# A feed-forward block on one core: w1's first piece on ScalarE's queue, the rest of w1 on SyncE's behind the table load, the bias by software DMA

## The chip, the cores and the metric

The kernel runs on one core of a Trainium2 chip. The metric is the device time of a run in microseconds (us), median over runs.

## The reference

Activations of 2048 tokens by 448 features go through a two-layer feed-forward block with a tanh-approximated GELU between the layers, all in bf16:

```python
def reference(x, w1, b1, w2, b2):
    h = jnp.einsum("bsd,df->bsf", x, w1) + b1      # x: 1 x 2048 x 448, w1: 448 x 1792
    h = _gelu(h)
    return jnp.einsum("bsf,fd->bsd", h, w2) + b2   # w2: 1792 x 448
```

## The kernel before, in words

The 2048 tokens are worked through in four chunks of 512. For each chunk, layer 1 computes the hidden features transposed (features on partitions, tokens along the row), in 14 feature tiles of 128, two tiles to a pair, so seven pairs. ScalarE adds the bias and applies GELU while it moves each tile from PSUM to the SBUF buffer `g` (L267). Layer 2 then multiplies `g` with w2, token tile by token tile; VectorE adds b2 and SyncE stores the tile (L310, L273).

The contraction of layer 1 is 448 = 3 x 128 + 64. Every matmul works on 64 rows of the array, so two of them, one on the upper and one on the lower half, run at once. A pair's part "a" is 6 matmuls (three steps of 128 rows, one half for each of the two tiles), its part "b" 8: the other halves, and last the remainder step `k == KT` with the 64 rows that are left over. Those remainder rows of w1 lie in `w1r`, loaded into partitions 64 to 127 (`load_w1r`, L135 to L137); for the odd tile of each pair VectorE copies them to partitions 0 to 63 (L381, events "w1rU"), because there the other half of the array does the remainder step.

w1 arrives in pieces. `W1CUTS = (0, 4, 8, 14)` cuts its main 384 rows by feature tile: piece 0 holds tiles 0 to 3 (384 KB), piece 1 tiles 4 to 7 (384 KB), piece 2 tiles 8 to 13 (576 KB). `RCUTS = (0, 4, 14)` cuts the remainder rows: piece 0 holds tiles 0 to 3 (64 KB), piece 1 the rest (160 KB). In the first chunk the order of pairs is L0.a and L1.a (in two halves of 256 tokens), L0.b, L2.a, L1.b, L3.a, L2.b, L4.a, L3.b and so on. So TensorE needs first piece 0 of w1, at the end of L0.b piece 0 of the remainder rows, at L2.a piece 1 of w1, at the end of L2.b piece 1 of the remainder rows, at L4.a piece 2 of w1.

The first chunk of x comes as it is (`xn`, L153) and is turned by TensorE (L337, L358), with VectorE and ScalarE moving the results to `xT` (L344, L367). Until x is there, TensorE runs warm-up matmuls on constants (L190). The other three chunks come through transposing DMAs (L147).

The order of the work is written by hand. A small helper, `Program`, keeps one list of operations per engine: `op` appends a computation, `dma` a transfer, `barrier` a bare wait. Each operation has a list of events that it waits for and may carry an event that it fires when done; `emit` turns these into semaphores and writes the lists out, engine by engine, in their order. So on each queue everything stands behind what was appended before it, a wait included.

At the start the queues hold:

- SyncE: x; w1 piece 0; w1 piece 2; remainder rows 1; w2 in two halves; b2; twelve transposing loads of x.
- ScalarE: the bias b1 (L171, waiting for VectorE's memset of its buffer, L170); a dummy GELU (L173), in front of which the activation table is loaded; remainder rows 0; w1 piece 1; then its evacuations.
- GpSimd: the identity matrix for the turning (L165, L166) and a memset for layer 2's bias rows (L169).
- VectorE: the memset; the evacuations of x; `turn_b1`, four 32x32 transposes and a cast that bring b1 onto partitions (L179, L181); the two remainder copies (L381); then the additions of layer 2.

Of the kernel before, what the change touches and what calls it, by code (L numbers as in the profile page):

```python
# [5 lines left out]
ACT = mybir.ActivationFunctionType  # L6
# [67 lines left out]
def bass_standalone__dense_activation_gelu__prompt_kernel(  # L74
# [10 lines left out]
    P = 128  # L85
# [5 lines left out]
    NSC, NST, STC, NFT = S // SC, S // P, SC // P, F // P  # L91
# [6 lines left out]
    with ExitStack() as es:  # L98
# [8 lines left out]
        junk = sb("junk", [P, 1], BF16)  # L107
        b1n = sb("b1n", [32, P], BF16)
# [8 lines left out]
        pr = Program(nc, es)  # L117
        one = nc.const_aps.tensor(1.0, [P, 1], BF16)
# [9 lines left out]
        def load_w1(i, engine="sync"):  # L128
            c0, c1 = W1CUTS[i] * P, W1CUTS[i + 1] * P
            pr.dma(engine, lambda e: e.dma_start(  # L130
                w1_sb[:, :, c0:c1], w1[0:D3, c0:c1].rearrange("(k p) f -> p k f", p=P)), ("w1", i))
# [3 lines left out]
        def load_w1r(i, engine="sync"):  # L135
            cs = slice(RCUTS[i] * P, RCUTS[i + 1] * P)
            pr.dma(engine, lambda e: e.dma_start(w1r[H:P, cs], w1[D3:D, cs]), ("w1r", i))  # L137

        def load_w2(a, b):
            pr.dma("sync", lambda e: e.dma_start(  # L140
                w2_sb[:, a:b, :], w2[a * P:b * P, :].rearrange("(f p) d -> p f d", p=P)), ("w2", a))
# [9 lines left out]
        x0v = x2[0:SC, :].rearrange("(p t) d -> p t d", t=STC)  # L151
        o0v = out2[0:SC, :].rearrange("(p t) d -> p t d", t=STC)
        pr.dma("sync", lambda e: e.dma_start(xn[:, :, :], x0v), "x")  # L153
        load_w1(0)
        load_w1(2)
        load_w1r(1)
        load_w2(0, 7)
        load_w2(7, 14)
        pr.dma("sync", lambda e: e.dma_start(b2_bc[:, :], b2.partition_broadcast(P)), "b2")
        for c in range(1, NSC):  # L160
            for slot in range(KT + 1):
# [6 lines left out]
            base=0, pattern=[[-1, P]], channel_multiplier=1), after=["ident0"], event="ident")  # L168
        pr.op("gpsimd", lambda e: e.memset(b2_z[:, :], 0.0), event="b2z0")  # L169
        pr.op("vector", lambda e: e.memset(b1n[:, :], 0.0), event="b1z")  # L170
        pr.dma("scalar", lambda e: e.dma_start(b1n[0:NFT, :], b1.rearrange("(c p) -> c p", p=P)), "b1n",  # L171
               after=["b1z"])
        pr.op("scalar", lambda e: e.activation(junk[:, :], one, ACT.Gelu_apprx_tanh))  # L173
        load_w1r(0, "scalar")
        load_w1(1, "scalar")

        def turn_b1():
            for q in range(4):
# [216 lines left out]
        for c in range(NSC):  # L395
# [14 lines left out]
            p = Layer2(c, (0, 1))  # L410
# [46 lines left out]
```

## Time and profile before

| what | us |
|---|---|
| median of 3 runs | 99.45 |
| lowest, highest | 99.04, 99.66 |
| the profiled execution, its own time | 99.45 |
| its span, first to last instruction | 98.1 |
| TensorE matmul busy | 92.4 (94% of the span) |
| ScalarE busy | 38.6 (39%) |
| VectorE busy | 13.4 (14%) |
| GpSimd busy | 1.1 (1%) |

The profile is of one execution. "PE" is TensorE's matmul side and "PEld" its weight loads, "DVE" VectorE, "ACT" ScalarE, "POOL" GpSimd, "SP" SyncE; a "q" behind a name is the engine's sequencer, which issues the DMAs. An issue row's length is the time of the issuing alone; the time to landing is given apart. In the names, `w_sb` stands for `w1_sb` and `w2_sb`, `u` for the PSUM units, `b_bc` for the broadcast b2, `b_f` for the turned b1. The page's slices show TensorE's granted clock in tenths over 40 equal stretches; for this run it begins:

```profile
PEclk9999957999999999999999999999999999999999
```

The mean granted clock of the run is 0.982.

### The profile page before, as it was taken

What the parts mean: (1) busy time and instruction counts of PE and PEld (TensorE: products, weight loads), DVE (VectorE), ACT (ScalarE), POOL (GpSimd) and SP (SyncE); (2) the same over time, 40 slices, a digit from 0 to 9 for tenths busy, and PEclk for the clock granted to TensorE, in tenths of its full rate; (3) what the DMA queues carried; (4) which work ended last, traced back from release to release, by engine and by line L of the source; (5) the groups of instructions that cost most, each with busy time, mean ns of one, the idle gap of its engine ahead of it and who ended that gap; (6) DMA issues with size and microseconds to landing.
All of it is one profiled execution on the core that took longest, in us unless ns stands there. A gap on an engine that the chain in (4) does not pass through costs nothing.

```text
span 98.1 us, 2060 instructions
## 1 busy us (share of the span) xinstructions
PE 92.4 (94%) x932; PEld 47.2 (48%) x932; DVE 13.4 (14%) x33; ACT 38.6 (39%) x63; POOL 1.1 (1%) x7
## 2 busy tenths in 40 slices
PE   6995399999999999999999999999999999999990
PEld 2571133445555444445555444455554444466890
DVE  0271101100004500000033300000044000000421
ACT  3262253894000088990000389870000698930001
POOL 4000000000000000000000000000000000000000
PEclk9999957999999999999999999999999999999999
DMA  2989999655422210000002300000002200000022
GB/s 64 304 281 308 359 269 124 127 98 102 103 60 76 71 41 0 0 7 0 0 0 97 96 0 3 0 0 7 0 19 74 94 7 0 0 0 7 0 94 94
DMA packets 12340, 7.32 MB, mean 75 GB/s; under 512 B 6956, under 2 KB 12140, under 8 KB 12332
## 3 DMA queue, kind: packets, MB, share of 16 engines
q1 hardware_dynamic: 11824, 6.74, 28.4%
q10 hardware_dynamic: 508, 0.46, 1.6%
q8 instruction: 7, 0.11, 0.5%
q14 instruction: 1, 0.01, 0.0%
HBM read 3.79 MB, written 1.84 MB: 57 GB/s over the span
## 4 chain that ended last, share of the span: by engine, by line
PE 86%; DMA 9%; ACTq 1%; ACT 1%; DVE 1%; issue 0%
PE u L215 86%; DMA w_sb<-in_w_dram 9%; ACTq L171 1%; ACT L173 1%; DVE out_sb L324 0%; DVE b1n L170 0%
## 5 line engine op out<-in xcount | busy, mean ns | idle before, releaser
L267 ACT ACTIVATE g<-u,b_f 128x512 bf16<-128x512 f32 x56 | 35.0, 686 | 44.9 <-PE u L215 44.9
L215 PE MATMUL u<-xT,w_sb 64*128 64x512 bf16 (+1 forms) x348 | 42.3, 378 | 2.0 <-DMA w_sb<-in_w_dram 2.0
L215 PE MATMUL u<-w_sb,g 64*128 64x448 bf16 (+1 forms) x504 | 43.2, 328 | 0.0
L215 PEld LDWEIGHTS u<-w_sb,g 64*128 64x128 bf16 x504 | 24.5, 94 | 18.4
L215 PEld LDWEIGHTS u<-xT,w_sb 64*128 64x128 bf16 x348 | 17.2, 96 | 22.4 <-DMA w_sb<-in_w_dram 2.3
L310 DVE TENSOR_TENSOR out_sb<-u,b_bc 128x448 bf16<-128x448 f32 x14 | 8.1, 620 | 64.9 <-PE u L215 64.9
L215 PE MATMUL u<-xT,w1r 64*128 64x512 bf16 x56 | 11.3, 391 | 0.7 <-DMA w1r<-in_w_dram 0.7
L215 PEld LDWEIGHTS u<-xT,w1r 64*128 64x128 bf16 x56 | 2.9, 96 | 4.7 <-DMA w1r<-in_w_dram 1.2
L190 PE MATMUL u<-const-bfloat16-1.0 128*128 128x512 bf16 (+1 forms) x9 | 3.8, 579 | 0.8 <-PEq L442 0.8
L327 ACT CAST out_sb<-u 128x224 bf16<-128x224 f32 x1 | 0.3, 347 | 9.2 <-PE u L215 9.2
L190 PEld LDWEIGHTS u<-const-bfloat16-1.0 128*128 128x128 bf16 x9 | 1.2, 141 | 2.4 <-issue 2.4
L173 ACT ACT_TABLE_LOAD x1 | 1.3, 1283 | 1.6 <-DVE b1n L170 1.6
L344 ACT COPY xT<-u 128x384 bf16<-128x384 bf16 x2 | 1.0, 479 | 2.0 <-PE u L337 2.0
L337 PEld LDWEIGHTS u<-ident,xn 128*128 128x128 bf16 x12 | 1.2, 144 | 0.6 <-issue 0.6
L337 PE MATMUL u<-ident,xn 128*128 128x128 bf16 x12 | 1.4, 310 | 0.0
L185 DVE COPY xT<-xT 64x512 bf16<-64x512 bf16 x3 | 0.9, 290 | 3.5 <-DMA xT<-in_x_dram 3.4
L381 DVE COPY w1r<-w1r 64x256 bf16<-64x256 bf16 (+1 forms) x2 | 0.6, 288 | 3.1 <-DMA w1r<-in_w_dram 3.1
L318 DVE TENSOR_TENSOR out_sb<-u,b_bc 128x448 bf16<-128x448 f32 x1 | 0.6, 625 | 1.7 <-PE u L215 1.7
L179 DVE STREAM_TRANSPOSE b1t<-b1n 32x32 bf16<-32x32 bf16 x4 | 0.8, 202 | 0.1
L405 DVE COPY b_z<-b_bc 1x448 bf16<-1x448 bf16 x1 | 0.3, 267 | 4.0 <-DMA b_bc<-in_b_dram 4.0
L344 DVE COPY xT<-u 128x384 bf16<-128x384 bf16 x2 | 0.7, 358 | 0.7 <-PE u L337 0.7
L367 ACT COPY xT<-u 64x256 bf16<-64x256 bf16 x2 | 0.7, 368 | 0.1
(17 smaller groups left out, 4.1 us busy)
## 6 DMA issues: line engine op xcount, KB each, us to landing
out_dram<-out_sb SPq DMA_DIRECT2D x16, 112.0 KB, 1.7
w_sb<-in_w_dram SPq DMA_DIRECT2D x2, 784.0 KB, 10.9
w_sb<-in_w_dram SPq DMA_DIRECT2D x1, 576.0 KB, 8.4
xn<-in_x_dram SPq DMA_DIRECT2D x1, 448.0 KB, 3.2
w_sb<-in_w_dram SPq DMA_DIRECT2D x1, 384.0 KB, 4.3
w_sb<-in_w_dram ACTq DMA_DIRECT2D x1, 384.0 KB, 9.1
xT<-in_x_dram SPq DMA_TRANSPOSE x12, 3.6
w1r<-in_w_dram SPq DMA_DIRECT2D x1, 160.0 KB, 8.8
```

The costliest lines, as they stand in the source:

```text
L171: pr.dma("scalar", lambda e: e.dma_start(b1n[0:NFT, :], b1.rearrange("(c p) -> c p", p=P)), "b1n", after=["b1z"])
L173: pr.op("scalar", lambda e: e.activation(junk[:, :], one, ACT.Gelu_apprx_tanh))
L179: pr.op("vector", lambda e, q=q: e.transpose(b1t[32 * q:32 * q + 32, :], b1n[:, 32 * q:32 * q + 32]), after=["b1n"], event=("b1t", q))
L185: pr.op("vector", lambda e: e.tensor_copy(xT[0:H, KT, s0:s1], xT[H:P, KT, s0:s1]), after=after, event=event)
L190: pr.op("tensor", lambda e: e.matmul(unit[0][:, 0, 0:cols], lhsT=ones_w, rhs=ones_m[:, 0:cols], start=True, stop=True))
L215: o = pr.op("tensor", lambda e: e.matmul(unit[u][:, lo, cols], lhsT=lhsT, rhs=rhs, start=start, stop=stop, skip_group_check=skip), after=a ...
L267: pr.op("scalar", lambda e, lo=lo, ft=ft: e.activation(g[:, ft, c * SC:(c + 1) * SC], unit[u][:, lo, :], ACT.Gelu_apprx_tanh, bias=b1_f[:, ...
L310: pr.op("vector", lambda e, lo=lo, j=j: e.tensor_tensor(out=out_sb[:, j, :], in0=unit[u][:, lo, 0:D], in1=b2_bc[:, :], op=ALU.add), after= ...
L318: pr.op("vector", lambda e: e.tensor_tensor(out=out_sb[:, j, :].rearrange("p (two h) -> p two h", two=2), in0=unit[u][:, :, 0:DH], in1=b2_ ...
L337: pr.op("tensor", lambda e, k=k: e.transpose(stage(t)[:, k * P:(k + 1) * P], xn[:, t, k * P:(k + 1) * P], ident[:, :]), after=["ident", "x ...
L344: pr.op(engine, lambda e: e.copy(o, i) if engine == "scalar" else e.tensor_copy(o, i), after=[("xt", t)], event=("xT0", t))
L367: e.copy(o, i) if engine == "scalar" else e.tensor_copy(o, i),
```

## The change

x is still first on SyncE's queue. Behind it stands a wait for the event "table", which the dummy GELU on ScalarE now fires when it is done. Behind the wait come remainder rows 0, w1 piece 1, remainder rows 1, w1 piece 2, and then w2, b2 and the transposing loads as before. w1 piece 0 is issued from ScalarE's queue, behind the table load and the dummy GELU; the other two w1 transfers leave that queue. The bias is loaded by a DMA issued from GpSimd's queue, behind its three preparing operations, with the same wait for VectorE's memset. Nothing else is touched: the same bytes are loaded, and TensorE's order of work is the same.

```diff
         pr.dma("sync", lambda e: e.dma_start(xn[:, :, :], x0v), "x")
-        load_w1(0)
+        pr.barrier("sync", ["table"])
+        load_w1r(0)
+        load_w1(1)
+        load_w1r(1)
         load_w1(2)
-        load_w1r(1)
         load_w2(0, 7)
         load_w2(7, 14)
...
         pr.op("vector", lambda e: e.memset(b1n[:, :], 0.0), event="b1z")
-        pr.dma("scalar", lambda e: e.dma_start(b1n[0:NFT, :], b1.rearrange("(c p) -> c p", p=P)), "b1n",
+        pr.dma("gpsimd", lambda e: e.dma_start(b1n[0:NFT, :], b1.rearrange("(c p) -> c p", p=P)), "b1n",
                after=["b1z"])
-        pr.op("scalar", lambda e: e.activation(junk[:, :], one, ACT.Gelu_apprx_tanh))
-        load_w1r(0, "scalar")
-        load_w1(1, "scalar")
+        pr.op("scalar", lambda e: e.activation(junk[:, :], one, ACT.Gelu_apprx_tanh), event="table")
+        load_w1(0, "scalar")
```

## The prediction

> **What bounds the kernel now.** I read the chain of waits in order of time first. It names the one wait that sets the end:
>
> ```profile
> 2.23 9.07 DMA w_sb<-in_w_dram
> 11.30 0.05 issue
> 11.35 84.59 PE u L215 x877
> 95.94 0.38 DVE out_sb L324
> ```
>
> From 11.35 us on it is TensorE alone. What released it is the second piece of w1 (feature tiles 4 to 7), issued at 2.23 on ScalarE's queue, behind the bias and the first remainder rows, and landed 9.07 later at 11.30. Next, the timeline from 0 to 20 us (start, length, engine, line; not every row):
>
> ```profile
> 5.83 2.13 PE L215 MATMUL u<-xT,w_sb 64*128 64x256 bf16 x30
> ...
> 8.68 0.64 PE L215 MATMUL u<-xT,w1r 64*128 64x512 bf16 x2 [0.71 <-DMA w1r<-in_w_dram]
> ...
> 11.35 1.58 PE L215 MATMUL u<-xT,w_sb 64*128 64x512 bf16 x12 [2.03 <-DMA w_sb<-in_w_dram]
> ...
> 16.07 1.46 PE L215 MATMUL u<-xT,w_sb 64*128 64x512 bf16 x12
> ...
> 17.58 1.46 PE L215 MATMUL u<-xT,w_sb 64*128 64x512 bf16 x12
> ```
>
> Layer 1 starts at 5.83, runs out of operands at 7.96, gets the remainder rows at 8.68 and w1's second piece at 11.35. Then there is a second loss: 28 matmuls between 11.35 and 16.07 take 4.72, while the 14 from 16.07 take 1.51, so 28 should take 3.02. The table by windows says why (after the stretch and its length: busy time of PE, PEld, DVE, ACT, POOL; then granted clock, DMA share, GB/s):
>
> ```profile
> 12.50:13.00 0.50, 0.50 (x6) 0.19 (x4) 0.00 (x0) 0.00 (x0) 0.00 (x0) 0.58 1.08 377
> 15.50:16.00 0.50, 0.50 (x4) 0.15 (x2) 0.09 (x1) 0.00 (x0) 0.00 (x0) 0.51 1.40 275
> 16.00:16.50 0.50, 0.50 (x7) 0.20 (x4) 0.00 (x0) 0.23 (x1) 0.00 (x0) 1.00 4.32 56
> ```
>
> A mean of 0.58 in the first half microsecond means full speed for 0.08 of it (0.16 + 0.84 x 0.5 = 0.58): the clock halves at 12.58 and is back at 15.99, 3.41 later. In the 3.41 before 12.58 TensorE was busy only 0.15 + 1.23 = 1.38 (40%). So the wait for w1 costs its own idle time and 4.72 - 3.02 = 1.70 of half clock.
>
> The page's part on DMA issues gives the order of landing:
>
> ```profile
> w_sb<-in_w_dram SPq DMA_DIRECT2D x1, 576.0 KB, 8.4
> xn<-in_x_dram SPq DMA_DIRECT2D x1, 448.0 KB, 3.2
> w_sb<-in_w_dram SPq DMA_DIRECT2D x1, 384.0 KB, 4.3
> w_sb<-in_w_dram ACTq DMA_DIRECT2D x1, 384.0 KB, 9.1
> ...
> w1r<-in_w_dram SPq DMA_DIRECT2D x1, 160.0 KB, 8.8
> ...
> w1r<-in_w_dram ACTq DMA_DIRECT2D x1, 64.0 KB, 7.0
> ```
>
> With the issue times of the timeline: x 0.73 to 3.93, w1 piece 0 1.19 to 5.5, piece 2 (576 KB, used last) 1.67 to 10.1, remainder rows 0 1.68 to 8.7, remainder rows 1 2.18 to 11.0, piece 1 2.23 to 11.3. Landing follows the order of issue across both queues: the big piece that is used last was asked for before the two that are used next.
>
> **What the Trainium skill says.** "DMA: Bandwidth & Descriptors", section "Issuing engines are not separate DMA queues": transfers from all queues run on the same 16 engines and interleave. The trace agrees: the two queues' landings form one sequence. The same page, "Anatomy of one DMA — SWDGE (gpsimd) path", prices a software DMA at about 2.0 us plus bytes over 436 GB/s; no row of this trace shows one. "TensorE: Matmul & The Clock Gate", Part 1, has the clock set by TensorE's activity in a free-running window of 3.41 us; the half-clock stretch measured here is 3.41. "SBUF — State Buffer", section "SBUF: two separate sides", warns that VectorE in a two-port mode can keep GpSimd from writing a software DMA's descriptors.
>
> **The change part by part.** All against the profiled execution: span 98.1, its own time 99.45 (1.35 around the span), which is also the median of the three runs.
>
> 1. ScalarE. The bias DMA (0.62 of issue, 0.95 to 1.57) and its wait for VectorE's memset go. The table load, held to 1.60 by them, can start at about 0.8: 1.28 of load, 0.20 of the dummy activation, so "table" fires at about 2.3 to 2.4. Piece 0's DMA is issued 0.08 after the load's start (as the 1.68 one was after 1.60), because the queue's sequencer does not wait for the load: at about 0.9 instead of SP's 1.19. ScalarE's next work is the evacuation at 4.89, so nothing there is later.
>
> 2. x and piece 0 now come on two queues at once. Below: no delay of x. Above: byte-equal sharing, x done with piece 0, whose landing is 5.5: 1.6 late. In between: x has 128 packets of 3.5 KB; if one 1 KB packet of piece 0 goes between each two, 128 KB come ahead of x's last, at about 310 GB/s (the 2 to 4 us window has 308) 0.4 us. I take 0.4. The turning of x and layer 1 start move from 5.83 to 6.2; piece 0 (832 KB with x, 5.5 before, at most 5.9 with some sharing) is there.
>
> 3. SP. The wait for "table" holds everything behind it: remainder rows 0, piece 1, remainder rows 1, piece 2, w2 twice, b2, the twelve transposing loads of x. First issue at about 2.4; at 0.55 each (0.48 to 0.60 in the rows) the four w1 DMAs go out at 2.4, 2.95, 3.5, 4.05, w2 to about 5.9. No hole in the stream: x and piece 0 keep the engines until about 4.6, and first bytes come about 1 us after an issue (x: 0.73, bytes from 1.75). Landing from this trace's own rate, 832 KB at 5.5 and all 2016 KB of x and w1 at 11.3, 204 KB/us (w2's early bytes in it, so not flattering): rows 0 at 896 KB, 5.8; piece 1 at 1280, 7.7; rows 1 at 1440, 8.5; piece 2 at 2016, 11.3. b2's issue already sits 5.33 on a full queue (4.20 to 9.53), and w2 landed by 15.0 for a use from 21.5 on (about 17 later), x's next chunk by 19.0 for a use at 32.1 (27.6 later): the later issues are hidden by that slack.
>
> 4. What TensorE needs. From the start S: 24 matmuls of 256 columns and 6 of 512, in pairs, S + 1.94 by the 0.108 and 0.216 per column pair that 1.51 per 14 matmuls gives; then the remainder step, which VectorE's copy of the rows holds to about S + 2.1 (turning the bias ends at S + 1.84, the copy takes 0.22), then piece 1 at S + 2.4. With S = 6.2: rows 0 needed at 8.1 (lands 5.8), piece 1 at 8.6 (7.7), rows 1 with its 0.35 copy at about 11.4 (8.9), piece 2 28 matmuls, 3.02, after 8.6, at 11.6 (11.3). All hold, the last by only 0.3.
>
> 5. Bias by software DMA. POOL is free at 1.87, after its last memset. Price by the skill: landed at 1.87 + 2.0 to 3, so 3.9 to 4.9; before, the bias's small packets moved at 3.0 to 4.0. VectorE asks for it at 6.45 + 0.4. VectorE is idle from 0.92 to 3.94, so the port warning does not bite. I take 0, covered by 2 us of slack.
>
> Sum: piece 1 used at 8.6 instead of 11.35: 2.75 gained. The following 3.41 windows are over 85% busy, so the half clock at 12.58 goes: 1.70 gained. The rest is the same dense TensorE stream and drain. 99.45 - 4.45 = 95.0.
>
> **The rivals.**
> - *Late start with a cold array.* The warm-up runs at 0.42 per 512 columns and layer 1 at 0.216: the array reached full speed about 5.8, a window boundary (12.58 less twice 3.41). The window from 2.34 holds 1.79 of warm-up, then transposes. If x comes 0.4 to 1.6 later, that window is emptier and full speed may wait to 9.17: about 3.0 of layer 1 at half speed costs 1.5, so 96.5; with x at its upper bound (1.2 more, 2.0 instead of 3.0 at half speed, 1.0) 97.2. For it: 1.79 is only 52%. Against: the transposes and filler still fill most of it.
> - *A wait moved on.* Piece 2 lands later than 11.3 plus its 0.3 of slack, by 1 to 1.5, since its issue is 2.4 later than before. 96.0 to 96.5. Against: its bytes queue behind 1440 KB that need until 8.5 anyway.
> - *Not faster: the bias comes late.* VectorE is in order: four bias transposes and the cast (1.22 with their gaps), then the remainder copy (0.22) that TensorE's remainder step waits for. If the bias lands at T, that step's copy ends at T + 1.44 against S + 2.1 = 8.3, so TensorE loses T - 6.9; a hole over 2 us brings back 1.70 of half clock. It eats the 4.45 from T = 9.7 on; at T = 11, 4.1 + 1.7 gives 100.8. For it: a 64 KB DMA issued at 1.68 landed 7.0 later here, and no software DMA is in this trace. Against: T would be 7.8 after POOL is free.
> - *No effect*, piece 1 landing as late as before, would leave 99.45 less 0; it would need the order of issue not to govern the landing, against the rows above.
>
> **How the numbers follow.** Forecast as summed, 94.3 to 95.9: 0.58. Late start, 95.9 to 97.4: 0.20. A wait moved on: 0.10. Bias late or no effect, 98 to 102: 0.10. Better than 94.3 (x not delayed, remainder step not waiting for its copy): 0.02. Eight in ten lie within 94.3 to 97.3. A change of about 1% is what a measurement of this kernel can tell from none. Slower by more: 0.07 of the bias case's 0.10. Within 1%: its other 0.03, and 0.02 for the tails of the late start and the moved wait. Faster, below 98.45: the remaining 0.88.
>
> **What would show each step.** Right: the chain no longer holds a w1 transfer of 9 us; layer 1 starts at 6.0 to 6.4 and runs without a hole; granted clock 1.00 from 12 to 17; piece 1 landed before 8.6; the first layer-2 matmul at about 17.0 instead of 21.5. Wrong: VectorE waiting for the bias at the bias transposes after 7; TensorE waiting for w1 around 11.6; matmuls of 0.43 per pair after 6.2; x landing past 4.5.

## The result and the profile after

The changed kernel takes 94.49 us (median of 4 runs, 93.81 to 94.75; times without a unit are in us from here on) against 99.25 us of the kernel before in the same measurement (4 runs): a ratio of 0.9525, 95% interval 0.9435 to 0.9616. The profiled execution has a span of 93.4 us (98.1 before), its own time is 94.75 (99.45 before), and the mean granted clock is 1.00 (0.982 before). The forecast was 95.0.

The chain of waits of the changed kernel, in order of time:

```profile
...
0.78 3.36 PE u L191 x8
4.14 1.29 PE u L338 x12
5.43 0.21 PE u L359 x2
5.65 0.21 PE u L191
5.86 85.41 PE u L216 x909
91.27 0.38 DVE out_sb L325
```

No transfer is left in it. From the warm-up on (L191) the chain is TensorE's own work: turning x (L338, L359), a filler, then layers 1 and 2 (L216) in one piece. Before, a w1 transfer of 9.07 stood in this place, and TensorE's piece began at 11.35.

The timeline of the changed kernel at the places that the prediction named (start, length, engine, line):

```profile
0.74 1.28 ACT L175 ACT_TABLE_LOAD   x1 [0.74 <-PEq L443]
0.75 0.39 SPq L153 DMA_DIRECT2D xn<-in_x_dram  x1
0.80 0.45 ACTq L130 DMA_DIRECT2D w_sb<-in_w_dram  x1
1.82 0.65 POOL L173 DMA_DIRECT2D b1n<-in_b_dram  x1
2.27 0.55 SPq L137 DMA_DIRECT2D w1r<-in_w_dram  x1
...
5.79 2.52 PE L216 MATMUL u<-xT,w_sb 64*128 64x256 bf16 x30
6.39 0.90 DVE L180 STREAM_TRANSPOSE b1t<-b1n 32x32 bf16<-32x32 bf16 x4
8.15 0.38 PE L216 MATMUL u<-xT,w1r 64*128 64x512 bf16 x2
8.37 1.46 PE L216 MATMUL u<-xT,w_sb 64*128 64x512 bf16 x12
11.39 1.46 PE L216 MATMUL u<-xT,w_sb 64*128 64x512 bf16 x12
```

Piece 1 of w1 is used at 8.37 instead of 11.35, and the 28 matmuls that follow take 3.02 (8.37 to 11.39) instead of 4.72. The windows where the clock was halved (busy time of PE, PEld, DVE, ACT, POOL; then granted clock, DMA share, GB/s) now read:

```profile
12.50:13.00 0.50, 0.50 (x8) 0.26 (x6) 0.00 (x0) 0.36 (x1) 0.00 (x0) 1.00 1.10 359
15.50:16.00 0.50, 0.50 (x8) 0.26 (x6) 0.00 (x0) 0.38 (x1) 0.00 (x0) 1.00 5.18 206
```

The landings, from the page's part on DMA issues (KB, us to landing):

```profile
w_sb<-in_w_dram SPq DMA_DIRECT2D x1, 576.0 KB, 6.4
xn<-in_x_dram SPq DMA_DIRECT2D x1, 448.0 KB, 3.1
w_sb<-in_w_dram ACTq DMA_DIRECT2D x1, 384.0 KB, 4.2
w_sb<-in_w_dram SPq DMA_DIRECT2D x1, 384.0 KB, 4.1
...
w1r<-in_w_dram SPq DMA_DIRECT2D x1, 160.0 KB, 4.0
```

With the issue times: x at 3.9, piece 0 at 5.0, remainder rows 0 (issued 2.27) at 5.5, piece 1 (2.87) at 7.0, remainder rows 1 (3.48) at 7.5, piece 2 (4.02) at 10.4. The order is now that of use.

The kernel before, in 36 executions beside the experiments, had a mean granted clock of 1.00 in 7 (97.71 to 98.08), of about 0.983 in 24 (median 99.51) and of about 0.965 in 5 (100.76 to 101.14), while the changed kernel had 1.00 in all of its 10. A stretch of 3.41 at half clock in a span of 98.1 gives a mean of 0.983, and two give 0.965: it fits that the kernel before pays for none, one or two such stretches, at about 1.5 each. Where they fall was seen in one profiled execution.

### The profile page after: what moved, and what is told of

Read it like the earlier page. It is cut to its first block, busy times and chain, and to the rows that moved or that the text cites. A ratio compares the mean times of both kernels' runs of the same rounds, so it can differ in the third digit from the quotient of the medians.

```text
span 93.4 us, 2060 instructions
## 1 busy us (share of the span) xinstructions
PE 90.4 (97%) x932; PEld 46.5 (50%) x932; DVE 13.3 (14%) x33; ACT 38.5 (41%) x63; POOL 1.7 (2%) x8
## 4 chain that ended last, share of the span: by engine, by line
PE 97%; DVE 0%; issue 0%
PE u L216 91%; PE u L191 4%; PE u L338 1%; DVE out_sb L325 0%; PE u L359 0%
## 5 line engine op out<-in xcount | busy, mean ns | idle before, releaser
L216 PE MATMUL u<-w_sb,g 64*128 64x448 bf16 (+1 forms) x504 | 43.2, 328 | 0.0
L216 PE MATMUL u<-xT,w_sb 64*128 64x512 bf16 (+1 forms) x348 | 41.2, 372 | 0.0
L216 PEld LDWEIGHTS u<-w_sb,g 64*128 64x128 bf16 x504 | 24.4, 94 | 18.6
L216 PEld LDWEIGHTS u<-xT,w_sb 64*128 64x128 bf16 x348 | 16.9, 95 | 19.6 <-issue 0.3
L216 PE MATMUL u<-xT,w1r 64*128 64x512 bf16 x56 | 10.6, 376 | 0.0
L191 PE MATMUL u<-const-bfloat16-1.0 128*128 128x512 bf16 (+1 forms) x9 | 3.8, 578 | 0.8 <-PEq L443 0.8
L216 PEld LDWEIGHTS u<-xT,w1r 64*128 64x128 bf16 x56 | 2.7, 94 | 3.3
L191 PEld LDWEIGHTS u<-const-bfloat16-1.0 128*128 128x128 bf16 x9 | 1.2, 138 | 2.4 <-issue 2.4
L338 PEld LDWEIGHTS u<-ident,xn 128*128 128x128 bf16 x12 | 1.2, 140 | 0.5 <-issue 0.5
L338 PE MATMUL u<-ident,xn 128*128 128x128 bf16 x12 | 1.4, 307 | 0.0
```

What stands on the lines that cost most here:

```text
L191: pr.op("tensor", lambda e: e.matmul(unit[0][:, 0, 0:cols], lhsT=ones_w, rhs=ones_m[:, 0:cols], start=True, stop=True))
L216: o = pr.op("tensor", lambda e: e.matmul(unit[u][:, lo, cols], lhsT=lhsT, rhs=rhs, start=start, stop=stop, skip_group_check=skip), after=a ...
L338: pr.op("tensor", lambda e, k=k: e.transpose(stage(t)[:, k * P:(k + 1) * P], xn[:, t, k * P:(k + 1) * P], ident[:, :]), after=["ident", "x ...
```

## The experiments

**The order of use on one queue.** The kernel before, with all of w1 on SyncE's queue in the order of use; the two w1 loads leave ScalarE's queue:

```diff
         load_w1(0)
-        load_w1(2)
-        load_w1r(1)
+        load_w1r(0)
+        load_w1(1)
+        load_w1r(1)
+        load_w1(2)
...
-        load_w1r(0, "scalar")
-        load_w1(1, "scalar")
```

> The kernel before with nothing but SyncE's order changed: x, w1 piece 0, remainder rows 0, piece 1, remainder rows 1, piece 2, w2; the bias stays on ScalarE's queue, no wait, no w1 transfer on ScalarE's queue. My theory (the order of issue governs the landing, the queues do not): piece 1 lands at about 7.5, no hole before layer 1's third pair, granted clock 1.00 throughout, time 94.0 to 95.2, the same as the changed kernel within 0.5. Rival (the gain comes from the second queue and the wait, which leave x and piece 0 alone on the engines): piece 1 later than 8.5, a hole stays, 96 or more.

Measured: 94.31 (93.98 to 94.62), the changed kernel's time. There is no wait for the table, and the bias is where it was: piece 1, issued at 2.25, landed at 7.5; layer 1 began at 5.91 and ran without a hole (no idle time of TensorE behind it), with the clock at 1.00. So the rearrangement of w1's loads is enough for the whole gain. Piece 0 on a second queue, the wait and the software DMA add nothing to it together. The edit does two things at once, though: it puts the loads into the order of use, and it takes two of them off ScalarE's queue.

**The same with the bias by software DMA.** All of w1 on SyncE's queue in the same order, without the wait, and the bias issued from GpSimd.

> SyncE's order alone (x, piece 0, remainder rows 0, piece 1, remainder rows 1, piece 2, no wait) and the bias by software DMA; ScalarE issues no load at all. If order is the whole of it and the bias is hidden either way, this is the same as the order alone and as the changed kernel: 94.0 to 94.8. If the software DMA costs or gains something by itself in that order, it moves by more than 0.4.

**The changed kernel once more**, on the same chip as this and as the two kernels further down:

> The changed kernel once more, beside the three that follow on the same chip: 94.2 to 94.8, with x landed by 4.0 and granted clock 1.00. It is the yardstick for the two differences of a few tenths.

Measured: one queue with software DMA 94.19 (93.96 to 94.81), changed kernel 94.22 (93.98 to 94.37). They are the same. The bias, by software, landed 3.9 after its issue in the one and 3.4 in the other, in time for both.

**The big piece first.** In the changed kernel, pieces 1 and 2 of w1 change places.

```diff
         load_w1r(0)
-        load_w1(1)
+        load_w1(2)
         load_w1r(1)
-        load_w1(2)
+        load_w1(1)
```

> The changed kernel with pieces 1 and 2 of w1 swapped on SyncE's queue (remainder rows 0, piece 2, remainder rows 1, piece 1). My theory: piece 1 is now the last of 2016 KB and lands at about 10.4 (where piece 2 landed in the changed kernel), needed at 8.2: a hole of about 2.2, and the half clock comes back if a window falls on it (up to 1.7): 96.7 if it does not, 98.4 if it does. Rival (the queue and not the order holds w1 back): piece 1 lands near 8.5, under 95.5.

Measured: 95.90 (95.71 to 96.20), 1.4 more than the changed kernel. Its timeline, at the hole:

```profile
8.26 0.38 PE L216 MATMUL u<-xT,w1r 64*128 64x512 bf16 x2
9.78 1.47 PE L216 MATMUL u<-xT,w_sb 64*128 64x512 bf16 x12 [1.15 <-DMA w_sb<-in_w_dram]
```

The hole is back behind the remainder step, as the order says, but with 1.15 of idle it is smaller than the 2.2 expected: piece 1, last of 2016 KB, landed at 9.7 and not at 10.4. The clock stayed at 1.00; a hole of this size did not halve it in any of the 4 executions.

The kernel before had piece 1 last of the same 2016 KB too, and there it landed at 11.3, with idle of 0.71 and 2.03. What differs is the queue. The packets moved up to the last ones of piece 1, in the kernel before (to 10.76; q1 is SyncE's queue, q10 ScalarE's) and in this one (to 9.11):

```profile
q1 hardware_dynamic: 1688, 2.20, 67.1%
q10 hardware_dynamic: 508, 0.46, 14.7%
...
q1 hardware_dynamic: 1260, 1.81, 68.6%
```

x and w1 on q1 come to 1.61 MB in the first and to 1.67 MB in the second; what is left, about 0.6 and 0.14 MB, is w2, issued after piece 1. In the kernel before, w2 on SyncE's queue moved beside piece 1 on ScalarE's, which fits a landing 1.6 later. So by this reading piece 1 was late for two reasons, the order and the second queue. What each is worth alone is not separated: no kernel here has the order of use with the two loads left on ScalarE's queue.

**The hole filled, no load moved.** The kernel before, with nine filler matmuls (results overwritten by L2.a) where TensorE waits:

```diff
         L[0].b()
+        for _ in range(9):
+            pr.op("tensor", lambda e: e.matmul(unit[2][:, 0, :], lhsT=ones_w, rhs=ones_m, start=True, stop=True),
+                  after=free(2))
         L[2].a()
```

> The kernel before with nine filler matmuls on constants (512 columns each, into a PSUM unit that is free) between L0.b and L2.a, where TensorE waits for w1's second piece from 9.3 to 11.3. No load moves. My theory (the hole costs its own time and, apart from that, 1.70 of half clock after it): piece 1 still lands at about 11.3, the granted clock stays 1.00, the 28 matmuls after it take 3.0 instead of 4.7: about 1.7 faster than before, 97.6. Rival (the slow 28 matmuls are slow for another reason, such as the traffic of the DMAs or PSUM): same as before, 99.3.

Measured: 98.23 (97.94 to 100.61) beside 99.75 for the kernel before (97.81 to 101.14). The timeline of the filled kernel:

```profile
9.55 2.14 PE L389 MATMUL u<-const-bfloat16-1.0 128*128 128x512 bf16 x9
11.75 1.47 PE L215 MATMUL u<-xT,w_sb 64*128 64x512 bf16 x12
13.06 0.38 PE L215 MATMUL u<-xT,w1r 64*128 64x512 bf16 x2
13.28 1.46 PE L215 MATMUL u<-xT,w_sb 64*128 64x512 bf16 x12
14.57 0.38 PE L215 MATMUL u<-xT,w1r 64*128 64x512 bf16 x2
14.79 1.46 PE L215 MATMUL u<-xT,w_sb 64*128 64x512 bf16 x12
```

Piece 1 is as late as ever (11.71), but the 28 matmuls behind it take 3.04 (11.75 to 14.79), not 4.72, with the same transfers going on. So traffic or PSUM does not make them slow. Three of the four executions had clock 1.00, against 1 of 7 for the kernel before beside it; they took 97.94 to 98.30, no less than the kernel before at clock 1.00, so the filler takes away the half clock and nothing else. The fourth, 100.61, still had 0.982, and where its half clock fell is open, since only one execution was profiled; an idle of 0.95 before the remainder step is left in this kernel.

**The bias late.** The changed kernel, its bias DMA held until piece 1 has landed:

```diff
-               after=["b1z"])
+               after=["b1z", ("w1", 1)])
```

> The changed kernel with the bias's software DMA held until w1's piece 1 has landed (about 7.0), so that the bias lands at T of 9.0 to 10.4. The prediction's rival says: VectorE is held at the bias transposes, its remainder copy ends at T + 1.44, TensorE's remainder step, at 8.15 in the changed kernel, waits for it: a loss of T - 6.7, 2.3 to 3.7, and up to 1.7 of half clock on top: 96.8 to 99.9. If instead nothing hangs on the bias until the first GELU's result is used, the loss stays under 1: below 95.5.

Measured: 102.24 (102.21 to 102.74). The chain of this kernel:

```profile
7.83 4.80 DMA b1n<-in_b_dram
12.66 0.20 DVE b1t L180
...
13.90 0.23 DVE w1r L382
14.18 85.08 PE u L216 x868
```

This is the prediction's slower case, made real: bias, VectorE's transposes, its remainder copy (L382), then TensorE, idle for 6.39. The size of T was missed: the software DMA, issued into the full stream, took 4.80 and landed at 12.63. The half clock lasted two windows here:

```profile
11.50:12.00 0.50, 0.00 (x0) 0.00 (x0) 0.00 (x0) 0.00 (x0) 0.00 (x0) 0.62 1.08 369
18.00:18.50 0.50, 0.50 (x6) 0.23 (x4) 0.00 (x0) 0.50 (x2) 0.00 (x0) 0.56 0.59 133
```

By these means it began at 11.62 (0.24 + 0.76 x 0.5 = 0.62) and ended at 18.44. TensorE worked in it from 14.18 on, which cost about 4.26 / 2 = 2.1, not the 1.7 of the kernel before. The mean clock was 0.966. With the measured T the rule gives a loss of 12.63 - 6.7 = 5.9 and, with 1.7, a time of 94.5 + 7.6 = 102.1; that this meets the 102.24 so well is partly luck, since the idle was 6.39, the half clock cost 2.1, and layer 1 had begun 0.35 earlier than in the changed kernel's profile.

**The bias back on ScalarE's queue.** The changed kernel, with the bias DMA ahead of the table load again:

```diff
-        pr.dma("gpsimd", lambda e: e.dma_start(b1n[0:NFT, :], b1.rearrange("(c p) -> c p", p=P)), "b1n",
+        pr.dma("scalar", lambda e: e.dma_start(b1n[0:NFT, :], b1.rearrange("(c p) -> c p", p=P)), "b1n",
```

> The changed kernel with the bias put back on ScalarE's queue ahead of the table load. The table load starts at 1.6 again, piece 0 is issued at 1.7, SyncE's wait ends at about 3.1. My theory (moving the bias is worth little): the engines have x until 3.2, so piece 0 lands at 5.2 to 5.6, piece 1 issued at 3.7 at about 7.8, still before 8.2: 94.5 to 95.0. Rival (the software DMA is a needed part): the later wait makes a hole in the stream, piece 1 lands at 8.5 to 9, TensorE waits 0.3 to 0.9: 95.3 or more.

Measured: 95.63 (95.30 to 96.12). My theory missed and the rival had the time right, though not the size of the delay: piece 1 landed at 9.68, and TensorE waited 0.62 for piece 0 and 1.21 for piece 1. Two things are mixed here, piece 0 issued at 1.67 instead of 0.80 and SyncE's wait ending at 3.13 instead of 2.27. The next kernel separates them.

**SyncE's wait lengthened.** The changed kernel, waiting for x too; bias and piece 0 stay where they are.

```diff
-        pr.barrier("sync", ["table"])
+        pr.barrier("sync", ["table", "x"])
```

> The changed kernel with SyncE's wait lengthened from the table (2.3) to the landing of x (about 3.9); the bias and piece 0 stay where they are. It separates what was mixed when the bias went back to ScalarE, where SyncE's wait ended at 3.1 and piece 0 was issued at 1.7. If the late wait empties the stream, the engines run dry when piece 0 is through at about 4.5, piece 1, issued at 4.5, lands at 8.7 to 10.4, needed at 8.2: 0.5 to 2.2 lost, 95.0 to 96.7. If it was piece 0's late issue, piece 1 still lands near 8 and the time stays under 94.9.

Measured: 95.58 (95.34 to 95.69) beside the changed kernel's 94.22. The windows of this kernel:

```profile
4.00:4.50 0.50, 0.50 (x6) 0.48 (x6) 0.17 (x1) 0.00 (x0) 0.00 (x0) 1.00 0.82 277
4.50:5.00 0.50, 0.50 (x9) 0.50 (x7) 0.36 (x1) 0.11 (x1) 0.00 (x0) 1.00 0.02 5
5.00:5.50 0.50, 0.46 (x7) 0.24 (x5) 0.40 (x2) 0.50 (x2) 0.00 (x0) 1.00 0.17 31
```

The last column is the point: the stream ran dry, 5 and 31 GB/s in a full microsecond, because piece 0 was through and what stood behind the wait had only just been issued: rows 0, issued at 4.00, moved their first packet at 5.34. Piece 1, issued at 4.61, landed at 8.74; TensorE idled 0.80 for it. So a later end of SyncE's wait is enough by itself to cost 1.4; what piece 0's later issue adds was not tried alone. In the kernel with the bias on ScalarE the stream also ran thin, at 59 GB/s from 3.5 to 4.0 and at 72 from 5.5 to 6.0.

**Without the wait.** The changed kernel, its barrier and the event taken out:

```diff
-        pr.barrier("sync", ["table"])
...
-        pr.op("scalar", lambda e: e.activation(junk[:, :], one, ACT.Gelu_apprx_tanh), event="table")
+        pr.op("scalar", lambda e: e.activation(junk[:, :], one, ACT.Gelu_apprx_tanh))
```

> The changed kernel without SyncE's wait for the table (and without the event). My theory: the wait is worth nothing, since SyncE's order already has the early pieces first and ScalarE issues piece 0 at 0.8, before SyncE's second transfer at about 1.2; remainder rows 0 and piece 1 land a little earlier, piece 0 at 5.0 to 5.5, layer 1 starts at 5.8: 94.5, within 0.4 of the changed kernel. Rival (the wait protects piece 0): SyncE's 448 KB of remainder rows and piece 1 share the engines with piece 0, which lands at 6 to 6.8; layer 1 starts up to 1 later, 95.2 or more.

Measured: 94.88 (94.56 to 95.03), on one chip with the order on one queue at 94.31. Piece 0 landed at 5.6 and was not the cause, so the rival's reason fails. x landed at 4.39. I took that for the reason and ran the kernel again:

> The changed kernel without SyncE's wait, once more. If the wait protects x, which landed at 4.4 without it and at 3.9 with it, it is slower than the changed kernel by about 0.4: 94.7 to 95.1, with x landing at 4.3 or later. If that was chance, it is the same as the changed kernel: 94.2 to 94.7, x by 4.1.

Measured: 95.08 (94.73 to 95.40) beside the changed kernel's 94.22. So the loss repeats, but x landed at about 3.9 this time. The chain of the second run names something else:

```profile
1.83 5.38 DMA b1n<-in_b_dram
7.23 0.20 DVE b1t L179
...
8.47 0.23 DVE w1r L381
8.76 82.99 PE u L215 x868
```

In this run it is the bias: landed at 7.2, TensorE idle 1.19 before its remainder step. In the first run it had landed at 6.9, when VectorE, late with x, asked for it at 6.92. The software queue's packets moved between 4.5 and 6.5 in both runs, and between 4.0 and 4.5, but for two, in the changed kernel. A last kernel takes the wait away and the bias off the software queue, to ScalarE's behind piece 0. Against the kernel without the wait:

```diff
-        pr.dma("gpsimd", lambda e: e.dma_start(b1n[0:NFT, :], b1.rearrange("(c p) -> c p", p=P)), "b1n",
+        load_w1(0, "scalar")
+        pr.dma("scalar", lambda e: e.dma_start(b1n[0:NFT, :], b1.rearrange("(c p) -> c p", p=P)), "b1n",
                after=["b1z"])
         pr.op("scalar", lambda e: e.activation(junk[:, :], one, ACT.Gelu_apprx_tanh))
-        load_w1(0, "scalar")
```

> The changed kernel without SyncE's wait and with the bias no longer by software DMA but on ScalarE's queue behind piece 0. Without the wait the software DMA landed the bias at 6.9 and 7.2 (5.2 with it), and TensorE's remainder step waited for it. If that is all that the wait protects, this kernel has the changed kernel's time: 94.0 to 94.6, VectorE turning the bias at 6.0 to 6.5 without waiting. If the wait also protects x or piece 0 by itself, it stays at 94.7 or more, with layer 1 starting at 6.2 or later.

Measured: 94.42 (94.15 to 94.78). VectorE turned the bias at 6.32 without waiting and layer 1 began at 5.71, though x landed at 4.1 again. With the bias off the software queue, all but 0.2 of the 0.9 is back. So the wait's main use appears to be to let the software DMA through before transfers on both hardware queues fill the engines. A direct harm to x from the missing wait, of some tenths, was seen in two of three profiles without it (4.39, 4.14, 3.9), but the big-piece kernel, which has the wait, also had x at 4.06: it is not settled.

## Why the prediction was right

It was right in direction and size, and in the main in its mechanism: 94.49 for 95.0, and the profiled span fell by 4.7 for the 4.45 of the sum. Two of its terms missed and cancelled. By its steps:

1. *ScalarE.* Table load at 0.74 (said 0.8), SyncE free at 2.27 (2.4), piece 0 issued at 0.80, 0.06 after the load's start (0.9). Right.
2. *x and piece 0 share the engines: x 0.4 late.* Wrong here. x landed at 3.9, as before. The q10 queue, which carries piece 0, moved its first packet between 3.0 and 3.1, when 103 of x's 128 had begun by 3.0 and 14 more began in that tenth. I had let packets alternate one by one. The Trainium skill ("DMA: Bandwidth & Descriptors", section "Queues, rings and completion order") has an engine drain a whole packet of several descriptors from one queue before it switches; if x's 128 are spread evenly, 8 to each of 16 engines, they could be one such packet each, and this landing would fit. No run tests it, and the last kernel speaks against it as a rule: there x and piece 0 were both issued at 0.73, q10 began at 2.85 with 79 of x's packets begun, and x landed at 4.14.
3. *The start of layer 1.* It began at 5.79, not 6.2, but its first 30 matmuls took 2.52 against 2.13 before: the 24 of 256 columns had a mean of 315 ns against 270. Pairs began every 0.21 up to 6.62 and every 0.11 from there on, so the array was still at half pace for the first part. This is the cost that the cold-start rival names, 0.39 instead of 1.5, but not by its reason: x was not late. In the second profile of the same kernel, with x landed at 3.8 as well, the 30 took 2.13. Over the seven profiles whose trace has a clock record, that record begins, at full speed, anywhere from 4.09 to 6.64, with x landed at 3.8 to 4.1 in all of them; where it begins at 6.64, in the big-piece kernel, the 30 took 2.42. So when full speed begins differs between executions, and x does not set it. The windows table says 1.00 there, as it does during the warm-up at 0.42 per matmul: the pace has to be read, not this figure. That the two misses cancel, 0.4 of x not lost and 0.39 of clock lost, is luck of this execution.
4. *Landings.* Said 5.8, 7.7, 8.5, 11.3 for remainder rows 0, piece 1, remainder rows 1, piece 2; measured 5.5, 7.0, 7.5, 10.4. The rate taken from the kernel before, 204 KB/us, was too low: w2's early bytes were in it, as the prediction says, and they were about 0.6 MB. Piece 2's thin slack of 0.3 was in truth 1.0 (used at 11.39). The first matmul of layer 2 came at 16.79 (said 17.0).
5. *The hole and the half clock.* 11.35 - 8.37 = 2.98 for the 2.75 of the sum, and 1.70 for 1.70: together 4.68. That the second term hangs on the idle time is borne out by the counts: half clock in 29 of 36 executions of the kernel before (idle 0.71 and 2.03), in 1 of 4 of the filled kernel, in 4 of 4 with the bias late (6.39), and in none of 50 of the kernels whose profile shows no idle over 1.21. But it is a term of most executions, not of all: the kernel before without any half clock takes about 97.9, so the hole alone is worth about 3.5 (in the profiled execution of the changed kernel 0.39 of it was lost to the cold start) and the clock about 1.5 in four executions of five.
6. *The bias.* Said 3.9 to 4.9, landed at 5.2; VectorE asked at 6.39. The cost was 0, as taken, but the cover was 1.2 and not 2, and it hangs on SyncE's wait: without it the bias landed 1.7 and 2.0 later, and in one of the two profiles TensorE lost 1.2 by it. The price used for it, about 2.0 plus the time of the bytes (the Trainium skill, "DMA: Bandwidth & Descriptors", section "Anatomy of one DMA — SWDGE (gpsimd) path"), was too low in every run: 3.4 here, 3.9 with all of w1 on SyncE's queue, 5.1 and 5.4 without the wait, 4.8 in the full stream.

What the prediction did not say: that w1's order on SyncE's queue is enough for the whole change. Its reading "landing follows the order of issue across both queues" pointed there, since by it one queue would do as well, but it was too simple: remainder rows 0, issued just after piece 2, landed 1.4 before it, and about 0.6 MB of w2 moved before the end of piece 1, which had been issued first. Of the other parts, the wait needs the bias out of its way (95.63 with it), and the software DMA beside two loaded queues needs the wait (94.88 and 95.08 without); neither is needed when both are left out. No version tried beats the changed kernel by more than the runs' spread.

## What to carry to other kernels

When an engine waits for a transfer, list all transfers with their issue and landing times first. If a big one that is used later was issued earlier, or one on another queue moves beside it, try a single queue in the order of use: here that alone gave the whole gain. Price the clock as well as the hole, and look at the granted clock of every execution, since a stretch at half clock may come and go between runs. A small software DMA that stands ahead of a critical copy needs its landing checked under the full load, because what is issued beside it moved it by up to 2 us here.

## What the runs showed of the hardware that was not expected

- A DMA of 3.5 KB by software took 3.3 to 5.4 to land, by what the hardware queues had been given, though its 32 packets counted for 0.0% of the engines in the page of the changed kernel.
- A second queue's transfer, issued 0.05 after x, moved nothing for 2.3 (0.80 to 3.08), until 112 of x's 128 packets had begun; x's own first packet came 1.02 after its issue.
- About 0.6 MB of a transfer moved before the end of one that had been issued earlier on another queue (w2 and piece 1 in the kernel before).
- Full speed of the array began between 4.09 and 6.64 in seven profiles, with the same warm-up and nearly the same x.
- After 6.39 of idle the first 15 matmuls took 2.96 (14.18 to 17.14), where 14 take 1.51 at full pace: half pace again.
